# The second of two MLPs in blocks of 768 tokens, its first layer by Strassen's algorithm; its weights widened earlier, attention's steps further apart

## Chip, cores and metric

One core of a Trainium2 chip runs the whole program. The metric is the device time of one execution, in microseconds. PE is TensorE, DVE VectorE, ACT ScalarE, POOL GpSimd; SP issues the DMAs.

## The reference

Linear attention over 8 batches, 8 heads, 576 tokens of 64 channels, then two MLPs over the 4608 tokens of 512 channels, with 2048 channels between. Weights come as float64.

```python
def _attn_ref(q, k, v):
    q_s = np.exp(q - np.max(q, axis=-1, keepdims=True))
    q_s = q_s / (np.sum(q_s, axis=-1, keepdims=True) + 1e-09)
    k_s = np.exp(k - np.max(k, axis=2, keepdims=True))
    k_s = k_s / (np.sum(k_s, axis=2, keepdims=True) + 1e-09)
    kv = np.einsum('bhsd,bhse->bhde', k_s, v)
    return np.einsum('bhsd,bhde->bhse', q_s, kv)
...
x = attn_out.transpose(0, 2, 1, 3).reshape(B * S, H * D)
h = x @ w_in;  r = np.maximum(h, 0.0);  y = (r * r) @ w_out            # first MLP
h = y @ w_in2;  g = h * (1.0 / (1.0 + np.exp(-1.702 * h)));  out = g @ w_out2
```

## The kernel before

Every large product takes both operands as hi + lo (hi rounded to float32r, lo the rest) and adds three products, hi hi, hi lo and lo hi, in PSUM. So one step of either layer on a 128x128 piece of weights is three matmuls of 512 columns. Tokens go through in 9 blocks of TB = 512. For each block and each of 16 chunks f of the middle channels, `first` (L450) makes 12 matmuls into a tile `ph`, `steps_g` (L468) turns it into g (ACT's Relu or Sigmoid L475/L477, a DVE multiply L483, `to_hi` on ACT L120, `to_lo` on POOL L123), and `second` (L497) adds 12 matmuls into four `acc` banks, LAG = 2 chunks behind. The first MLP runs over all blocks and leaves y in DRAM; `plan_y` brings it back for the second MLP, which runs the same loops.

PSUM has eight banks: four for `acc`, two for `ph` (pool `ps_h`), two for attention (`ps_at`).

Attention works on a pair of heads at a time, one block ahead of the MLP. Its steps, with the names used below: km (DVE, maximum over k), pt (PE transposes km), mt (DVE), pb (PE spreads mt), ke (DVE subtracts, ACT takes exp), pk (PE, k times v), r, kvn, kvh, kvl; and for q: qs (DVE maximum and sum), POOL's subtraction and multiplication, qt (16 DVE transposes, L377), qh (ACT), ql (DVE), px (PE, L414), xh and xl. Per block there are four pairs.

Weights are widened from float64 words by `steps_w` (L136): a load, ACT's Abs (L160), three DVE bit steps (L165, L168, L171), then hi on ACT and lo on POOL. Those of the second MLP follow during block 8 and after it, in the place of the first MLP's.

The order is written in two ways. Up to block 1 it is the hand-written list ORDER. After that each step has a time in us (`at`), counted in half slots HS = 2.6, and steps are emitted in order of time; the lists KV1, X1 and W1 (L98 to L100) hold the times of attention's steps and of the weights. Each engine runs its instructions in that order. SP issues all DMAs, in order, and waits there for what a DMA needs.

## Time and profile before

| | us |
|---|---|
| median of 3 runs (lowest to highest) | 1727.88 (1727.25 to 1729.3) |
| span of the profiled execution | 1726.0 |
| PE busy in it | 1677.2 (97%) |
| DVE, ACT, POOL busy | 770.9, 594.2, 562.0 |
| PE's chain: first layers L460, second layers L509 | 37%, 35% of the span |

The page is one execution. Matmuls overlap in it: a matmul of 512 columns is listed with 0.39 us, and the next starts 0.23 us after it, so counts in a window say more than durations. "Idle before" is the time that an engine stood still ahead of an instruction, with what ended it.

### The profile page before, as it was taken

How to read it: one execution, taken by the hardware profiler on the slowest of the kernel's cores; microseconds unless marked ns; L12 is line 12 of the kernel's file. 1: busy time of each engine (PE TensorE's matmuls, PEld its weight loads, DVE VectorE, ACT ScalarE, POOL GpSimd, SP SyncE). 2: the span in 40 equal slices, each digit the busy share in tenths (PEclk: the TensorE clock that was granted, in tenths of full speed). 3: DMA queues.
4: the chain of work that ended last, by engine and by line, in shares of the span. 5: the costliest groups of instructions: out<-in, count | busy, mean ns of one | idle time of the engine just before them, and what ended most of it. 6: DMA issues, size and time to landing. Idle time of an engine off the chain costs nothing.

```text
span 1726.0 us, 19815 instructions
## 1 busy us (share of the span) xinstructions
PE 1677.2 (97%) x7560; PEld 1384.2 (80%) x7560; DVE 770.9 (45%) x1360; ACT 594.2 (34%) x1030; POOL 562.0 (33%) x470
## 2 busy tenths in 40 slices
PE   6789999999999999999999999999999999999999
PEld 5568888888888888878887888888888888888887
DVE  8995555656554655544368752121212121212111
ACT  5654333333333333333245432222222222222222
POOL 4665323333233323323245542222222222222222
PEclk9989999999999999999999999999999999999999
DMA  7552212121110202110234420000101010101000
GB/s 208 163 148 85 52 27 67 38 63 42 47 44 24 81 27 60 28 37 13 79 92 143 129 80 22 26 24 22 29 15 35 8 42 2 48 1 43 1 25 25
DMA packets 103712, 92.52 MB, mean 54 GB/s; under 512 B 51905, under 2 KB 85697, under 8 KB 103617
## 3 DMA queue, kind: packets, MB, share of 16 engines
q1 hardware_dynamic: 103616, 91.25, 18.0%
q8 instruction: 59, 0.97, 0.2%
q14 instruction: 37, 0.29, 0.1%
HBM read 72.35 MB, written 18.87 MB: 53 GB/s over the span
## 4 chain that ended last, share of the span: by engine, by line
PE 74%; DVE 17%; ACT 4%; issue 3%; DMA 1%; POOL 1%; SPq 0%; DVEq 0%; ACTq 0%; POOLq 0%
PE ph L460 37%; PE acc L509 35%; DVE qt L377 6%; DVE ql L123 2%; DVE to L168 1%; PE px L414 1%; ACT qh L120 1%; DVE ti L168 1%; DVE g L483 1%; DVE to L165 1%; DVE ti L165 1%; DMA rawi<-in_moe_w_in_dram 1%; ACT kvn L297 1%; DVE ti L171 1%; ACT g L475 1%
## 5 line engine op out<-in xcount | busy, mean ns | idle before, releaser
L123 POOL TENSOR_TENSOR g<-g,g 128x512 fp32r<-128x512 f32 x288 | 377.6, 1311 | 986.1 <-ACT g L120 887.1
L460 PE MATMUL ph<-xh,wih 128*128 128x512 f32 x1152 | 453.8, 394 | 0.1
L460 PE MATMUL ph<-xl,wih 128*128 128x512 f32 x1152 | 449.1, 390 | 0.4 <-DVE xl L123 0.4
L460 PE MATMUL ph<-xh,wil 128*128 128x512 f32 x1152 | 449.3, 390 | 0.0
L509 PE MATMUL acc<-g,woh 128*128 128x512 f32 x1152 | 361.6, 395 | 2.5 <-ACT g L475 1.8
L509 PE MATMUL acc<-woh,g 128*128 128x512 f32 x1152 | 356.7, 391 | 3.8 <-ACT o L523 3.8
L483 DVE TENSOR_TENSOR g<-ph,g 128x512 f32<-128x512 f32 x144 | 99.6, 692 | 528.4 <-ACT g L477 525.9
L120 ACT ACTIVATE g<-g 128x512 fp32r<-128x512 f32 x288 | 182.0, 632 | 274.5 <-DVE g L483 274.4
L509 PEld LDWEIGHTS acc<-woh,g 128*128 128x128 f32 x1152 | 217.3, 189 | 49.7 <-ACT o L523 4.2
L460 PEld LDWEIGHTS ph<-xh,wih 128*128 128x128 f32 x1152 | 217.1, 188 | 45.6 <-PE warm L594 0.2
L460 PEld LDWEIGHTS ph<-xh,wil 128*128 128x128 f32 x1152 | 216.6, 188 | 45.8
L509 PEld LDWEIGHTS acc<-g,woh 128*128 128x128 f32 x1152 | 214.1, 189 | 48.4 <-ACT g L475 2.7
L460 PEld LDWEIGHTS ph<-xl,wih 128*128 128x128 f32 x1152 | 216.8, 188 | 44.0 <-DVE xl L123 0.7
L477 ACT ACTIVATE g<-ph 128x512 f32<-128x512 f32 x144 | 86.1, 598 | 422.8 <-PE ph L460 422.8
L509 PE MATMUL acc<-g,wol 128*128 128x512 f32 x576 | 225.6, 392 | 0.5 <-POOL wol L123 0.5
L509 PE MATMUL acc<-wol,g 128*128 128x512 f32 x576 | 225.1, 391 | 0.0
L483 DVE TENSOR_TENSOR g<-g 128x512 f32<-128x512 f32 x128 | 91.8, 717 | 202.1 <-ACT g L475 199.7
L475 ACT ACTIVATE g<-ph 128x512 f32<-128x512 f32 x144 | 85.9, 597 | 217.2 <-PE ph L460 215.9
L377 DVE STREAM_TRANSPOSE qt<-q 32x128 f32<-32x128 f32 x448 | 135.5, 303 | 7.9 <-POOL q L352 2.2
L509 PEld LDWEIGHTS acc<-g,wol 128*128 128x128 f32 x576 | 108.6, 189 | 24.3 <-POOL wol L123 1.0
L509 PEld LDWEIGHTS acc<-wol,g 128*128 128x128 f32 x576 | 108.6, 189 | 22.5
L123 DVE TENSOR_TENSOR xl<-yr,xh 128x512 fp32r<-128x512 f32 x36 | 45.6, 1267 | 43.7 <-ACT xh L120 43.7
(67 smaller groups left out, 1124.1 us busy)
## 6 DMA issues: line engine op xcount, KB each, us to landing
rawi<-in_moe_w_in_dram SPq DMA_DIRECT2D x32, 512.0 KB, 3.8
rawo<-in_moe_w_out_dram SPq DMA_DIRECT2D x32, 512.0 KB, 3.6
...
```

What stands on the lines that cost most here:

```text
L120: nc.scalar.activation(hi, src, AF.Copy)
L123: eng.tensor_tensor(out=lo, in0=src, in1=hi.bitcast(F32), op=ALU.subtract)
L165: nc.vector.tensor_scalar(out=t, in0=t, scalar1=3, scalar2=1, op0=ALU.logical_shift_left, op1=ALU.bitwise_or)
L168: nc.vector.scalar_tensor_tensor(out=t, in0=high, scalar=-0x80000000, in1=t, op0=ALU.bitwise_and, op1=ALU.bitwise_or)
L171: nc.vector.scalar_tensor_tensor(out=t, in0=low, scalar=29, in1=t, op0=ALU.logical_shift_right, op1=ALU.bitwise_or)
L297: nc.scalar.activation(kn[hs, hs], pk[hs, hs], AF.Copy, scale=r[hs])
L377: nc.vector.transpose(out=st["qt"][32 * g : 32 * g + 32, a * P : (a + 1) * P].rearrange("d (j t) -> d j t", j=QJ), in_=st["qn"][32 * a : 3 ...
L460: nc.tensor.matmul(ph, a[:, cs], x[:, c, :], start=(c == 0 and e == 0), stop=(c == NC - 1 and e == 2),)
L475: nc.scalar.activation(st["g"], st["h"], AF.Relu)
L477: nc.scalar.activation(st["g"], st["h"], AF.Sigmoid, scale=1.702)
L483: nc.vector.tensor_tensor(out=st["g"], in0=st["g"] if m == 0 else st["h"], in1=st["g"], op=ALU.mult)
L509: nc.tensor.matmul(acc, lhsT, rhs, start=(f == 0 and e == 0), stop=(f == NF - 1 and e == 2),)
```

## The change

**Second MLP.** Its tokens go in 6 blocks of 768 (two halves of TH = 384). The first layer takes the products of 2x2 blocks (two halves of the tokens, two halves of the input channels, two chunks of 128 middle channels) with seven block products in place of eight (`steps_l1`). One such piece of work, "a quad" here (`quad(n)`, n from 0 to 47), has seven products of six matmuls of 384 columns, spaced by PT = QT / 7 in the plan. Sums of x (s1 to s4, `steps_s`) and of weights (a, b, `steps_q`) are made once and split in hi and lo. Results are put together by DVE adds as the products appear (c11, c12, c21, c22), in two `ps_h` banks in turn. `unit` is one piece of the second layer: three matmuls of 512 columns; 12 of them, for the quad before, lie between the products. Six accumulators hold 768 tokens, the two attention banks being free by then.

**Weights of the second MLP** are widened during blocks 1 to 7 (`steps_w` with m = 1) and stored in DRAM as float32; block 8 loads those of the first layer, makes their sums and splits them. Those of the second layer are split in quads 0 to 7, stored as hi and lo, and loaded again for each later block of tokens (`load_o`).

**Attention.** KV1 and X1 have longer distances, and x of a block lies once, not twice, in SBUF: px is copied out (`x_out`) and split into hi and lo (`split_x`) just ahead of the block.

```diff
-    KV1 = [HS * t for t in (-4, -3.9, -0.9, 0.2, 1.1, 2.2, 3.1, 3.15, 4.2, 5.1, 5.1, 5.1, 5.1)]
-    X1 = [HS * t for t in (-2, 0.1, 0.1, 1.1, 2.1, 2.1, 3.6, 5.1, 5.1, 6.2, 7.1, 7.1)]
-    W1 = [HS * t for t in (-4, -1, 0, 1, 1)]
+    KV1 = [HS * t for t in (-4, -3.9, -0.9, 0.6, 1.5, 2.7, 3.5, 3.55, 5.6, 6.6, 6.6, 6.6, 6.6)]
+    X1 = [HS * t for t in (-2, 0.1, 0.1, 1.1, 2.1, 2.1, 4.0, 6.0, 6.0, 8.2, 9.0)]
+    QT = 15.4
+    PT = QT / 7
...
-    xpool = ctx.enter_context(tc.tile_pool(name="xpool", bufs=2))
+    xpool = ctx.enter_context(tc.tile_pool(name="xpool", bufs=1))
...
+    raws = Places(
+        [(wpool, f"i{NF - 5 - e}") for e in range(4)]
+        + [(wpool, f"o{NF - 1 - e}") for e in range(4)]
+        + [(xpool, "x6"), (cpool, "raw")]
+    )
...
+    def split_x(i, p):
+        new_x(i, p)
+        src = x_t.pop(("f", i, p))
+        to_hi(x_t[i, p][:, 0, :], src)
+        to_lo(x_t[i, p][:, 1, :], src, x_t[i, p][:, 0, :], nc.gpsimd if p % 2 else nc.vector)
...
+        def product(bank, x, begin):
+            def run():
+                if begin:
+                    st[bank] = ps_h.tile([P, TB], F32, tag="h", name=f"p{x}_{n}")
+                a, at0 = W_AT[x]
+                w, xs = wt[a, j], x_t["2", i, x]
+                for k in range(2):
+                    cs = slice(at0 + k * P, at0 + (k + 1) * P)
+                    three(st[bank][:, :TH], lambda e: w[:, e, cs], lambda e: xs[:, e, k, :], begin and k == 0, k == 1, shared=True)
...
+        return [
+            (0.0, product(0, "a11", True)),
+            (0.48, m1),
+            (1.0, product(1, "s2", True)),
+            (1.5, add("c12", 1, "m1")),
+            (2.0, product(0, "a12", False)),
+            (2.5, act("c11")),
+            (3.0, product(1, "s3", False)),
+            (3.1, split("c11")),
+            (3.5, add("c22", 1, "m1")),
+            (4.0, product(0, "s1", True)),
+            (4.5, add("c22", 0, "c22")),
+            (4.55, act("c22")),
+            (5.0, product(1, "a22", False)),
+            (5.1, split("c22")),
+            (5.5, add("c21", 1, "m1")),
+            (5.55, act("c21")),
+            (6.0, product(0, "s4", False)),
+            (6.1, split("c21")),
+            (6.5, add("c12", 0, "c12")),
+            (6.55, act("c12")),
+            (7.1, split("c12")),
+        ]
...
+        for n in range(2 * NF):
+            i, e = (1 + n // 5, n % 5) if n < 20 else (5 + (n - 20) // 4, (n - 20) % 4)
+            t = slot(i) + (4.2 + (5.6 if n < 20 else 6.8) * e) * HS
+            when(t, [HS * e for e in (0, 3.0, 3.4, 4.2, 5.0, 5.1)], steps_w("io"[n // NF], 1, n % NF))
...
+            at(t + 2.1 * HS, sums("a"))
+            at(t + 3.1 * HS, sums("b"))
+            for e, a in enumerate(("w1", "wa", "wq", "wb")):
+                if a != "wb" or j % 2 == 0:
+                    f, tag = next(tags)
+                at(max(t + (2.2 + 0.9 * e) * HS, slot(NB - 1, f + 1) + HS), split(a, tag))
...
+            else:
+                t = quad(NQ * i - 1)
+                times = [quad(NQ * i - 6) - t, quad(NQ * i - 3) + 0.7 * PT - t, quad(NQ * i - 2) + 0.7 * PT - t]
+                times += [0.6 * PT if i < 2 else quad(NQ * i - 2) + 3.7 * PT - t]
+                times += [e * PT for e in (0.5, 1.55, 2.55, 1.6, 3.6, 4.6, 5.6, 6.6)]
+                when(t, times, steps_s(i))
+        UNITS = [0, 0, 1, 1, 2, 2, 3, 3, 4, 4, 5, 6]
```

Three places of the order follow. The first is DVE, one pair of heads (attention for block 3, while the MLP is in block 2; g is the MLP's square, ti a weight being widened). DVE's rows before:

```order
L263 TENSOR_TENSOR ke_1_2587<-k_1_2387,pb_1_2568 128x2x5x64
L483 TENSOR_TENSOR g_2_6_2593<-g_2_6_2593 128x512
L377 STREAM_TRANSPOSE qt_1_2599<-q_1_2467 32x128 x16
L290 TENSOR_SCALAR r_1_2650<-pk_1_2628 128x1
L291 RECIPROCAL r_1_2650<-r_1_2650 128x1
L123 TENSOR_TENSOR ql_1_2660<-qt_1_2599,qh_1_2659 128x4x4x32
L483 TENSOR_TENSOR g_2_7_2663<-g_2_7_2663 128x512
L238 TENSOR_REDUCE km_2_2681<-k_2_2583 128x128
```

DVE's rows after, for the same pair, from the square of g5 on:

```order
L635 TENSOR_TENSOR g_5_2638<-g_5_2638 128x512
L414 TENSOR_TENSOR ke_1_2644<-k_1_2426,pb_1_2616 128x2x5x64
L528 STREAM_TRANSPOSE qt_1_2659<-q_1_2501 32x128 x16
L635 TENSOR_TENSOR g_6_2692<-g_6_2692 128x512
L137 TENSOR_TENSOR ql_1_2719<-qt_1_2659,qh_1_2718 128x4x4x32
L201 TENSOR_SCALAR ti_6_2704<-ti_6_2704 128x512
L389 TENSOR_REDUCE km_2_2723<-k_2_2631 128x128
L441 TENSOR_SCALAR r_1_2725<-pk_1_2698 128x1
```

The transposes stand ahead of the square of g6 that they followed, r and its reciprocal went behind ql, and a bit step of a weight (ti) came between ql and the next pair's km.

The second place is PE in the second MLP. Its rows before (ph the first layer, acc the second):

```order
L460 MATMUL ph_2_9_9238<-xh_2_8439,wil_9_7889 128x512
L460 MATMUL ph_2_9_9238<-xh_2_8439,wih_9_7887 128x512
L460 MATMUL ph_2_9_9238<-xl_2_8440,wih_9_7887 128x512
L460 MATMUL ph_2_9_9238<-xh_2_8439,wil_9_7889 128x512
L509 MATMUL acc_2_0_9022<-woh_7_7759,g_1_2_7_9190 128x512 x2
L509 MATMUL acc_2_0_9022<-wol_7_7761,g_1_2_7_9190 128x512
L509 MATMUL acc_2_1_9023<-woh_7_7759,g_1_2_7_9190 128x512 x2
```

PE's rows after, the first four products of quad 5 (pa and ps the products, gc the results of quad 4 that the second layer takes):

```order
L610 MATMUL pa_5_8650<-a_0_7544,w_7822 128x384 x6
L610 MATMUL acc_0_0_8147<-wo_0_8_8592,gc_4_8581 128x512 x3
L610 MATMUL acc_0_1_8151<-wo_0_8_8592,gc_4_8581 128x512 x3
L610 MATMUL ps_5_8670<-s_0_7592,wq_7865 128x384 x6
L610 MATMUL acc_0_2_8164<-wo_0_8_8592,gc_4_8581 128x512 x3
L610 MATMUL acc_0_3_8168<-wo_0_9_8622,gc_4_8619 128x512 x3
L610 MATMUL pa_5_8650<-a_0_7988,w_7822 128x384 x6
L610 MATMUL acc_0_4_8183<-wo_0_9_8622,gc_4_8619 128x512 x3
L610 MATMUL acc_0_5_8187<-wo_0_9_8622,gc_4_8619 128x512 x3
L610 MATMUL ps_5_8670<-s_0_7997,wa_7828 128x384 x6
```

Rows of 12 and 12 matmuls became products of six matmuls of 384 columns with one or two units of three matmuls of 512 between them.

The third place is POOL in block 8. Its rows before (g the lo part of the MLP's g, wol and wil of a weight):

```order
L123 TENSOR_TENSOR g_0_8_8_7320<-g_8_8_7317,g_0_8_8_7320 128x512
L123 TENSOR_TENSOR wol_1_7346<-to_1_7296,woh_1_7344 128x512
L123 TENSOR_TENSOR g_0_8_9_7367<-g_8_9_7364,g_0_8_9_7367 128x512
L123 TENSOR_TENSOR wil_2_7388<-ti_2_7340,wih_2_7386 128x512
L123 TENSOR_TENSOR g_0_8_10_7413<-g_8_10_7410,g_0_8_10_7413 128x512
L123 TENSOR_TENSOR wol_2_7418<-to_2_7370,woh_2_7416 128x512
L123 TENSOR_TENSOR wil_3_7454<-ti_3_7406,wih_3_7452 128x512
```

POOL's rows after, in the same block (w, wa, wq and wbb are the lo parts of the weights and of their sums):

```order
L137 TENSOR_TENSOR wq_7620<-tb_7575,wq_7620 128x512
L137 TENSOR_TENSOR g_8_7_7641<-g_7_7638,g_8_7_7641 128x512
L137 TENSOR_TENSOR wbb_7656<-tt_7503,wbb_7656 128x256
L137 TENSOR_TENSOR w_7659<-tt_7595,w_7659 128x512
L137 TENSOR_TENSOR g_8_8_7684<-g_8_7681,g_8_8_7684 128x512
L137 TENSOR_TENSOR wa_7699<-ta_7636,wa_7699 128x512
L137 TENSOR_TENSOR wq_7702<-tb_7662,wq_7702 128x512
L137 TENSOR_TENSOR wbb_7656<-tt_7595,wbb_7656 128x256
```

Between two lo parts of g stand one or two weight splits before, and two or three after.

## Rows read from the trace of the kernel before

**Rows 1.** The page, part 1: busy time of each engine (share) xinstructions.

```profile
PE 1677.2 (97%) x7560; PEld 1384.2 (80%) x7560; DVE 770.9 (45%) x1360; ACT 594.2 (34%) x1030; POOL 562.0 (33%) x470
```

**Rows 2.** Windows: busy us (xinstructions) of each engine, granted clock, DMA.

```profile
core 0: us, PE busy (x) PEld busy (x) DVE busy (x) ACT busy (x) POOL busy (x), PEclk, DMA share, GB/s
50.00:100.00 50.00, 39.47 (x165) 30.84 (x164) 49.00 (x56) 28.68 (x53) 32.64 (x24) 0.93 0.53 153
300.00:400.00 100.00, 98.51 (x465) 81.73 (x464) 54.49 (x126) 37.03 (x66) 31.35 (x29) 1.00 0.18 48
900.00:1000.00 100.00, 96.23 (x413) 79.15 (x412) 80.71 (x91) 49.41 (x86) 55.88 (x40) 0.97 0.44 137
1100.00:1200.00 100.00, 100.00 (x442) 82.79 (x442) 19.78 (x25) 25.86 (x43) 24.10 (x19) 1.00 0.07 22
```

**Rows 3.** Waits of PE, 150 to 850 and 850 to 1000: total, times, longest.

```profile
PE px L414 <- DVE ql L123: 10.0, 19, 0.6
...
PE acc L509 <- ACT o L523: 3.8, 1, 3.8
```

**Rows 4.** Timeline of one pair of heads, 388 to 402.

```profile
388.36 0.27 PE L252 MATMUL pb<-ident,mt 128*128 128x128 f32 x1
...
392.81 5.04 DVE L377 STREAM_TRANSPOSE qt<-q 32x128 f32<-32x128 f32 x16
...
399.21 1.11 ACT L120 ACTIVATE qh<-qt 128x512 fp32r<-128x512 f32 x1
...
400.35 1.09 DVE L123 TENSOR_TENSOR ql<-qt,qh 128x512 fp32r<-128x512 f32 x1 [2.11 <-ACT qh L120]
...
400.65 0.28 PE L414 MATMUL px<-qh,kvl 128*128 128x256 f32 x1
...
401.50 0.38 PE L414 MATMUL px<-ql,kvh 128*128 128x256 f32 x1 [0.57 <-DVE ql L123]
```

**Rows 5.** Timeline of PE: px with 384 columns, then 512 (203 to 206.5).

```profile
204.70 0.34 PE L414 MATMUL px<-qh,kvh 128*128 128x384 f32 x1
...
205.22 0.40 PE L460 MATMUL ph<-xh,wih 128*128 128x512 f32 x1
...
205.91 0.39 PE L460 MATMUL ph<-xh,wih 128*128 128x512 f32 x1
```

**Rows 6.** Timeline of weight loads (PEld) in px, 301.9 to 304.2.

```profile
303.21 0.19 PEld L414 LDWEIGHTS px<-ql,kvh 128*128 128x128 f32 x1 [0.76 <-DVE ql L123]
303.32 0.19 PEld L414 LDWEIGHTS px<-qh,kvh 128*128 128x128 f32 x1
```

**Rows 7.** Timeline of PE behind the wait at the passage, 943 to 946.6.

```profile
943.84 1.22 PE L509 MATMUL acc<-woh,g 128*128 128x512 f32 x2 [3.77 <-ACT o L523]
...
945.28 1.06 PE L509 MATMUL acc<-woh,g 128*128 128x512 f32 x2
```

**Rows 8.** Timeline of DVE and POOL while weights are widened, 880 to 889.

```profile
882.66 0.69 DVE L168 SCALAR_TENSOR_TENSOR ti<-rawi,ti 128x512 int32<-128x512 int32 x1
883.04 1.47 POOL L123 TENSOR_TENSOR g<-g,g 128x512 fp32r<-128x512 f32 x1 [3.08 <-ACT g L120]
...
883.39 1.67 DVE L171 SCALAR_TENSOR_TENSOR ti<-rawi,ti 128x512 int32<-128x512 int32 x1
...
884.47 1.75 POOL L123 TENSOR_TENSOR wol<-to,woh 128x512 fp32r<-128x512 f32 x1
```

**Rows 9.** Costliest groups: busy us, mean ns of one, idle before.

```profile
L123 POOL TENSOR_TENSOR g<-g,g 128x512 fp32r<-128x512 f32 x288 | 377.6, 1311 | 986.1 <-ACT g L120 887.1
L120 ACT ACTIVATE g<-g 128x512 fp32r<-128x512 f32 x288 | 182.0, 632 | 274.5 <-DVE g L483 274.4
...
L238 DVE TENSOR_REDUCE km<-k 128x128 f32<-128x640 f32 x32 | 41.7, 1303 | 1.3 <-DMA k<-in_k_dram 1.3
L168 DVE SCALAR_TENSOR_TENSOR to<-rawo,to 128x512 int32<-128x512 int32 x32 | 38.0, 1187 | 1.1
L171 DVE SCALAR_TENSOR_TENSOR to<-rawo,to 128x512 int32<-128x512 int32 x32 | 32.7, 1023 | 1.1
L165 DVE TENSOR_SCALAR to<-to 128x512 int32<-128x512 int32 x32 | 26.4, 825 | 6.7 <-ACT to L160 6.7
```

More of the change, by code (lines that the diff above doesn't have):

```diff
@@ L468, in steps_g, with three, first @@
-    def steps_g(m, i, f):
+    def three(out, w, x, start, stop, shared=False):
+        for e, (a, b) in enumerate(((0, 0), (0, 1), (1, 0))):
+            nc.tensor.matmul(
+                out, w(a), x(b), start=(start and e == 0), stop=(stop and e == 2), skip_group_check=shared
+            )
+    def first(i, f, chunks=range(NC)):
+        if chunks[0] == 0:
+            pool, tag = (ps_acc, f"acc{f}") if i == 0 and 2 <= f < OPEN else (ps_h, "h")
+            h_t[i, f] = pool.tile([P, TB], F32, tag=tag, name=f"ph{i}_{f}")
+        w = wt["i", f]
+        for c in chunks:
+            x, cs = x_t[i, c], slice(c * P, (c + 1) * P)
+            three(h_t[i, f], lambda e: w[:, e, cs], lambda e: x[:, e, :], c == 0, c == NC - 1)
@@ new lines, in put @@
+    def put(i):
+        if i < NB - 1:
+            both = cpool.tile([P, 2, TB], F32, tag="raw", name=f"o{i}")
+        for c in range(NC):
+            if c > 1 and i < NB - 1:
+                o = both[:, c - 2, :]
+            else:
+                o = cpool.tile([P, TB], F32, tag="tgtg"[c], name=f"o{i}_{c}", bufs=2)
+            if c % 2 == 0:
+                nc.scalar.activation(o, acc_t[i][c], AF.Copy)
+            else:
+                nc.vector.tensor_copy(o, acc_t[i][c])
+            nc.sync.dma_start(out=y_d[i][:, c, :], in_=o)
@@ new lines, with put_2 @@
+    at_once = []
+    more_o = {}
+    def put_2():
+        for i, tokens in at_once:
+            acc = acc_t["2", i][tokens][0]
+            if i < NB2 - 1 and tokens not in (2, 3):
+                o = late["pool"].tile([P, TB], F32, tag="o", name=f"o2_{i}_{tokens}", bufs=2)
+            elif i < NB2 - 1:
+                if tokens == 2:
+                    more_o[i] = cpool.tile([P, 2, TB], F32, tag="raw", name=f"o2_{i}")
+                o = more_o[i][:, tokens - 2, :]
+            else:
+                if i not in more_o:
+                    more_o[i] = late["pool"].tile([P, NT2, TB], F32, tag="xf", name=f"o2_{i}")
+                o = more_o[i][:, tokens, :]
+            if tokens % 2 == 0:
```

556 lines of the change are left out of this document (374 added, 182 removed).

## The prediction

> **What bounds the kernel now.** I read the page first, then the table of windows, the waits and the timelines. TensorE is busy for 1677.2 of the 1726.0 us [rows 1]. The windows say where the rest lies. In the second MLP (1100 to 1200) TensorE is busy all the time: 442 matmuls of 512 columns, one per 0.2262 us, at a granted clock of 1.00 [rows 2]. There only fewer columns can save time. In the first MLP (300 to 400) 1.5 us of 100 are lost; at the passage between the MLPs (900 to 1000) 413 matmuls ran where 442 fit, 29 x 0.2262 = 6.6 us; up to 150 VectorE is the bound (49.00 of 50 us) [rows 2]. The waits name the first two losses [rows 3]. From 150 to 850 the one wait is px for ql, 19 times, 10.0 us. Near 940 the one wait is acc for ACT's copy o, 3.8 us, and behind it matmuls run at half clock: a pair takes 1.06 us where 0.62 is usual [rows 7], which is the rest of the 6.6.
>
> **1. First layer of the second MLP.** Before: 9 x 16 x 12 = 1728 matmuls of 512 columns. After, by the code and the order: 48 units of work ("quads": 768 tokens, 256 channels) with seven products of 6 matmuls of 384 columns, 2016 in all. The second layer keeps its 1728 matmuls of 512. What does one of 384 columns cost? The trace has them, in threes, in px: starts at 204.70 and 205.22 are three apart, 0.173 us each; right behind, three of 512 columns (205.22 to 205.91) are 0.230 apart [rows 5]. The ratio is 0.7536, near 3/4, so I see no fixed part, and take 0.7536 x 0.2262 = 0.1704. Sum: 1728 x 0.2262 = 390.9 before, 2016 x 0.1704 = 343.5 after, **-47.4 us**. Bounds: -48.8 at exactly 3/4, -41.5 at 0.1733.
>
> Twice as many small accumulations need readers in between. In a quad PE runs product, units of the second layer (two, two, two, two, two, one, one, of 3 x 0.2262 = 0.68 us each), product of 1.02 us, and so on: 7 x 1.02 + 12 x 0.68 = 15.3 us. A product that goes on in a bank, or takes its buffer again, comes two steps behind the one before in it, so reader chains have 3.7 us (1.36 + 1.02 + 1.36), and 2.4 us (0.68 + 1.02 + 0.68) at the tightest, add c21 before the next quad's a11. An add of 384 columns is 3/4 of the 0.69 us of a 512 step [rows 8], 0.5 us as an estimate. That is covered, so the products cost nothing beyond their columns in an ordinary quad. In quad 0 there is no second layer of its own to fill in: after s3 ends, act c11 (sigmoid and multiply, about 1.2 us) has one product of 1.02 as cover, and add c21 similar: 0.3 + 0.3, with hand-overs **+1** (0 to 3).
>
> **2. Attention's steps spread.** The chain of one pair of heads now [rows 4]: pb at 388.36; 16 transposes on DVE from 392.81, 5.04 us; qh on ACT until 400.32; ql on DVE until 401.44; px waits, its third matmul starts 0.85 us after the second where 0.11 is usual. PE has four half slots of 12 matmuls (2.72 us each) and pk between pb and px. The order shows six after the change, 6 x 2.72 + 0.55 = 16.9 us. DVE's row there: square of g5 (waits for ph5: 2.72 + 0.7 + 0.7, so 4.2 us after pb), ke until 5.0, transposes until 10.0, square of g6 10.7, then ql, when qh (11.1) is there, until 12.3. So 4.6 us of cover, and the px waits go: 10.0 us by the waits, 19 x 0.74 = 14 by the starts, I take **-13**.
> What is late next: km of the next pair stands behind ql, and now behind b0 of a widened weight too (0.83 us), and takes 1.30 [rows 9]: done at 14.4, pt's turn on PE at 5 x 2.72 + 0.55 = 14.15. In that pair (one of four, in blocks 1 to 7) PE waits 0.2 us, or 1.2 if DVE has met a POOL step: **+1.5** (0 to 7 x 1.2 = 8). The other pairs have over 1 us left by the same count.
>
> **3. Weights widened in blocks 1 to 7.** The 32 chunks (on DVE 0.83 + 1.19 + 1.02 [rows 9]) are not more work, but move out of block 8 and beyond, where DVE was busy 80.71 of 100 us, into blocks where it is busy 54.49 [rows 2]: five of 3.0 us per block of some 95 us (384 x 0.2262 and attention's products), about 70. Hidden beside TensorE, but for the km above. Their loads and stores go through SP: a store waits there for DVE's last bit step, and loads of k and q queue behind it. Those loads are issued at least 2.1 half slots (5.5 us) ahead of use; I count nothing, up to 2.
> x has one buffer now. Block i's x is split after first(i-1,15) has read each quarter: two ACT steps of 0.63 and DVE or POOL steps of 1.3 per pair, while PE has 2.0 + 2.7 us before first(i,0) starts and 0.68 more per quarter: nothing, by 0.7 us at the least.
>
> **4. Block 8 and the passage.** The old wait of 3.8 with its half-clock stretch goes (**-6.6**), since its copies are no longer behind weights. But POOL and DVE now share block 8 with 32 splits, 16 g_lo, and the sums of x. The trace shows that steps of these two hold each other up where both DVE operands are in SBUF: an L171 of 0.69 us that begins during a POOL step ends 0.55 after that step (1.67), and the POOL step behind it takes 1.75 [rows 8]. Work: POOL 40 x 1.29 + 8 x 0.65 + three of 768 columns at 1.94 = 62.6; DVE squares 16 x 0.69, sums 8 x 1.43, three of 768 at 1.0 = 25.5; together 88.1 against 16 x 5.43 = 86.9 us of the block. As the rows hand over 0.14 us early each time, it is rather 77. g_lo has 10.9 us from ph to its use, less 0.63 + 0.69 + 0.63 + 1.31 [rows 9]: 7 us of cover for a backlog. I take **+1.5** for the last splits (a12, s1, s4 stand behind wa and wq on POOL), 0 to 7.
> The Trainium skill's page "SBUF — State Buffer" (section "SBUF: two separate sides") gives the rule: the pair of ports is an exclusive lock, held for the whole instruction. Rows 8 agree, with 1.67 for 0.69. By that rule at its full durations block 8 would be oversubscribed.
>
> **5. Boundaries of the 768-token blocks.** In quads 7, 15, 23, 31, 39 POOL has 4 x 0.98 + 4 x 1.94 = 11.7 us of 15.3 (quad 7 with two weight splits 14.3), and DVE's multiplies and x sums wait among them. The chain multiply c22, add c21, multiply c21, add c12 then ends about when the bank is wanted: **+3** (0 to 10).
>
> **6. Start and end.** DVE, the bound there, loses three subtractions of 0.69: **-1** (0 to -4, as raw weights have ten places in place of three). The end (last copy and store) is the same.
>
> **Sum** on the profiled execution: 1726.0 - 47.4 + 1 - 13 + 1.5 - 6.6 + 1.5 + 3 - 1 = 1665.0. The median of the runs shown, 1727.88, is 1.9 above that span: **1667 us**.
>
> **The rivals.**
> Ports: POOL and DVE hold each other up in block 8 and at the boundaries beyond their cover, PE stops for some us and then runs at half clock as at 943.84 [rows 7]. Price: 6.6 again at the passage, 5 x 2 at the boundaries, less the 4.5 already counted: 1679. For it: 88.1 of 86.9 above. Against: the 7 us of cover.
> Refill: the px waits come back elsewhere (km, mt, or a load behind a store on SP), as DVE goes from 54 to 70: +13, 1680. Against: the spread moves each of these steps apart too.
> Weight loads: each load lasts 0.19 us [rows 6], more than the 0.170 of a matmul of 384 columns; if it set the pace, 2016 x (0.188 - 0.1704) = +35, 1702. Against: in rows 6 loads of 0.19 start 0.11 apart, so they overlap. The page "Perfetto Trace Analysis" of the Trainium skill (section "Identifying the Most-Contended Engine") judges TensorE by the share of LDWEIGHTS; by it the second MLP would go from 83% to 78 x 0.188 / 15.3 = 96% and have little left, but no run yet shows such loads in a long row.
> Slower: in every quad PE waits for a bank, because a multiply with two SBUF operands meets a POOL step (1.6 in place of 0.5) ahead of add c21 and add c12, whose cover is 2.4 us. Slower than before from (1731 - 1667) / 48 = 1.35 us a quad; at 1.4 it is 1734. For it: rows 8. Against: POOL has 4 us of 15.3 in an ordinary quad.
> That the change doesn't do what it says is excluded: the order has 2016 matmuls of 384 columns and 1728 of 512 fewer.
>
> **How the numbers follow.** Forecast 0.67, ports 0.13, refill 0.08, weight loads 0.05, slower 0.05, and 0.02 for some sum of losses that ends within 0.2% (3.5 us, about what a measurement of this kernel can tell from no change). Low end: -48.8, -14, -6.6, -4, nothing new: 1654. High end: 0.1733 (+5.8), px only 10 (+3), attention +5, ports +12: 1693. Faster 0.93, same 0.02, slower 0.05.
>
> **What would show it.** Right: matmuls of 384 columns 0.170 apart in the second MLP, a quad in 15.3 us, no wait of px for ql after 200, nothing over 1 us at the passage. Wrong: 0.188 in their place; waits of PE for DVE's c or POOL's g in every quad; waits of pt for km; a granted clock under 1.00 near the passage.

## The result, and the profile of the changed kernel

The changed kernel takes 1698.15 us (median of 4 runs, 1697.46 to 1700.28), the kernel before 1727.57 on the same chip: a ratio of 0.9831, 95% interval 0.9817 to 0.9845. It is faster by 29.4 us, where 61 were forecast. The profiled execution has a span of 1696.8 us; the sum had given 1665.0. So 31.8 us are to be found.

The page's first part has TensorE busy for 97% of the span and VectorE, the next of the engines beside it, for 55%; it stands against [rows 1]:

```profile
PE 1645.3 (97%) x7848; PEld 1411.2 (83%) x7848; DVE 940.5 (55%) x1647; ACT 669.6 (39%) x1228; POOL 694.7 (41%) x589
```

The windows, in the columns of [rows 2], tell the stages apart. They are, in this order, attention beside the first MLP, the passage in two halves, and the second MLP:

```profile
300.00:400.00 100.00, 98.65 (x469) 81.87 (x468) 71.43 (x146) 41.15 (x74) 34.49 (x30) 1.00 0.29 86
850.00:900.00 50.00, 45.77 (x193) 36.80 (x192) 23.55 (x23) 17.45 (x33) 32.59 (x26) 0.97 0.20 68
900.00:950.00 50.00, 45.81 (x208) 39.16 (x207) 30.54 (x29) 23.82 (x44) 42.01 (x31) 0.97 0.26 85
1100.00:1200.00 100.00, 100.00 (x500) 89.93 (x498) 40.81 (x65) 35.85 (x68) 39.10 (x32) 1.00 0.21 77
```

In the second MLP TensorE never waits, and still does only 500 matmuls in 100 us: a quad has 78, so it takes 15.6 us, not 15.3. The timeline of TensorE there shows why (start, us, engine, line, operation, count):

```profile
1299.68 1.21 PE L610 MATMUL ps<-s,wa 128*128 128x384 f32 x6
1300.72 1.55 PE L610 MATMUL acc<-wo,gc 128*128 128x512 f32 x6
1302.11 1.21 PE L610 MATMUL ps<-s,wa 128*128 128x384 f32 x6
```

From start to start, six of 384 columns take 1300.72 - 1299.68 = 1.04 us, and six of 512 take 1.39. Over the stretch of 1120 to 1680 the mean from start to start is 0.1749 us at 384 columns and 0.2317 at 512, where the sum had 0.1704 and 0.2262. Both kinds of matmul became dearer.

The waits of PE, first 150 to 850, then 850 to 1000, against [rows 3] (total, times, longest):

```profile
PE pt L395 <- DVE r L441: 3.4, 6, 0.8
PE pt L395 <- DVE km L389: 2.6, 1, 2.6
...
PE pa L610 <- DVE c L796: 4.0, 1, 4.0
PE ph L610 <- ACT g L629: 3.1, 1, 3.1
PE acc L610 <- POOL g L137: 0.9, 1, 0.9
```

The px waits for ql are gone, waits of pt stand in their place, and the passage has two new waits of 3 and 4 us, each with a stretch at the lower of TensorE's two clock levels (1.2 for 2.4 GHz) behind it: the granted clock is 0.97 in both halves of the passage.

So the missing time lies in four places, by starts in the trace:

| stage | forecast | measured | missing |
|---|---|---|---|
| second MLP, 2016 x 0.1749 + 1728 x 0.2317 | 734.4 | 753.0 | 18.6 |
| passage and quad 0, above pure streams | 2.5 | 13.2 | 10.7 |
| attention, 150 to 850: 40 matmuls more than before, x 0.2262 | -11.5 | -9.0 | 2.5 |
| start, 0 to 150: 6 matmuls fewer | -1 | +1.3 | 2.3 |

The forecast of 2.5 for the passage is the +1.5 for the last splits and the +1 for quad 0. The four give 34.1, some 2 more than the 31.8 that are missing; I can't place those 2.

### The profile page after: what moved, and what is told of

The parts are those of the page before. It is cut to its first block, busy times and chain, and to the rows that moved or that the text cites. A ratio compares the mean times of both kernels' runs of the same rounds, so it can differ in the third digit from the quotient of the medians.

```text
span 1696.8 us, 21565 instructions
## 1 busy us (share of the span) xinstructions
PE 1645.3 (97%) x7848; PEld 1411.2 (83%) x7848; DVE 940.5 (55%) x1647; ACT 669.6 (39%) x1228; POOL 694.7 (41%) x589
## 5 line engine op out<-in xcount | busy, mean ns | idle before, releaser
L610 PE MATMUL acc<-wo,gc 128*128 128x512 f32 x1728 | 453.9, 394 | 0.0
L610 PE MATMUL acc<-g,wo 128*128 128x512 f32 x1728 | 425.2, 395 | 4.2 <-ACT g L629 1.6
L610 PE MATMUL ph<-x,wi 128*128 128x512 f32 x1728 | 425.4, 395 | 3.5 <-ACT g L629 3.1
L610 PEld LDWEIGHTS acc<-g,wo 128*128 128x128 f32 x1728 | 323.4, 190 | 74.0 <-POOL g L137 2.9
L610 PEld LDWEIGHTS ph<-x,wi 128*128 128x128 f32 x1728 | 322.6, 189 | 71.8 <-ACT g L629 3.5
L137 POOL TENSOR_TENSOR gc<-c,gc 128x384 fp32r<-128x384 f32 x192 | 199.5, 1040 | 437.4 <-ACT gc L134 430.5
L610 PEld LDWEIGHTS acc<-wo,gc 128*128 128x128 f32 x1728 | 319.8, 188 | 46.3
L137 POOL TENSOR_TENSOR g<-g,g 128x512 fp32r<-128x512 f32 x144 | 194.4, 1350 | 396.9 <-ACT g L134 352.2
L610 PE MATMUL pa<-a,w 128*128 128x384 f32 x576 | 117.7, 339 | 4.4 <-DVE c L796 4.0
L610 PE MATMUL ps<-s,wa 128*128 128x384 f32 x576 | 116.0, 335 | 0.7 <-DVE c L808 0.4
L610 PEld LDWEIGHTS ps<-s,wa 128*128 128x128 f32 x576 | 102.8, 188 | 10.2 <-DVE c L808 1.2
```

The costliest lines, as they stand in the source:

```text
L137: eng.tensor_tensor(out=lo, in0=src, in1=hi.bitcast(F32), op=ALU.subtract)
L610: nc.tensor.matmul(out, w(a), x(b), start=(start and e == 0), stop=(stop and e == 2), skip_group_check=shared)
```

## Experiments

The runs were made on several chips, on which the kernel before took 1726.9 to 1729.1 us. So each time is compared with that of the kernel before on the same chip ("difference"). A difference has an uncertainty of some 2.5 us, so where less is at stake I go by the traces.

### The price of a matmul in the second MLP

**e1: streams alone.** This program has nothing but matmuls, in rows of one width, then in the order of two quads, alone and beside each other engine.

> The kernel is left out but for its matmul shapes: TensorE runs streams of F32R matmuls one after the other, each from a line of its own, and no result is the reference's. Streams: 512 columns 12 to a bank; 384 columns 6 to a bank; 384 columns out of 512-wide operands; 512 columns 3 to a bank with weights out of a 384-wide tile; the products and units of two quads in the order of the changed kernel (84 of 384, 72 of 512), alone, with four units at a time, beside ScalarE, VectorE, GpSimd, and all three with transfers. Theory A (the price lies in TensorE's own stream): in the quads alone the mean start to start is 174 to 176 ns at 384 columns and 231 to 233 at 512, as in the changed kernel, while the pure streams stay near 170 and 226; the neighbours add nothing. Theory A' (the price comes from the neighbours): the quads alone run at 170.4 and 226.5 ns, 15.2 us a quad, and some 4 ns a matmul appear only in the streams beside ScalarE, VectorE, GpSimd or transfers, and that stream names the neighbour.

The timeline of TensorE: L63 and L68 are the 384 columns (L68 out of 512-wide operands), L73 the 512 in threes, L79 and L82 the two quads that begin at 100.44 and end at 129.03, where L88 starts:

```profile
45.33 16.83 PE L63 MATMUL bank<-x,W 128*128 128x384 f32 x96
62.00 16.80 PE L68 MATMUL bank<-X,W 128*128 128x384 f32 x96
78.64 21.96 PE L73 MATMUL bank<-W,G 128*128 128x512 f32 x96
100.44 2.27 PE L79 MATMUL bank<-x,W 128*128 128x384 f32 x12
102.54 1.55 PE L82 MATMUL bank<-W,G 128*128 128x512 f32 x6
...
129.03 3.30 PE L88 MATMUL bank<-x,W 128*128 128x384 f32 x18
```

A pure row of 384 takes (62.00 - 45.33) / 96 = 0.1736 us each, one of 512 (100.44 - 78.64) / 96 = 0.2271. In the quads, with no other engine at work, the means are 0.1749 and 0.2317: those of the changed kernel to the last digit. Beside ScalarE, VectorE, GpSimd and all three with transfers they stay at 0.1748 to 0.1749 and 0.2317 to 0.2318. Theory A holds in that the price lies in TensorE's own stream, and A' falls; but A had the pure rows near 170 ns, and 384 columns stand at 173.6 there. Four units at a time instead of two (L88 and L91) gave 0.1752 and 0.2300, so coarser groups win next to nothing.
The Trainium skill's page "SBUF — State Buffer" (section "SBUF: two separate sides") says that TensorE's own ports never wait for another engine; this run agrees, with 0.1749 us alone and 0.1748 to 0.1749 beside the others.

**e8: what in the order costs.** These are streams of the same kind, with one thing changed at a time.

> Only matmul streams again, no result: 512 and 384 columns alone; 6 and 6, 12 and 12, 24 and 24, 3 and 3, 42 and 36 of each in turn; the same alternation of operands and banks with both kinds at 512 columns, and with both at 384; 256 with 512 and 448 with 512. Theory (each change of width costs a fixed sum, some 35 to 45 ns for a pair of changes, spread over the first 9 or so matmuls behind it): the alternation at one width runs at the pure 227 and 173.5 ns; per pair of changes the excess is the same at 12 and at 24 and smaller where runs are shorter than 9; with 42 and 36 the mean comes within 1 ns of the pure streams. Rival (the price comes of changing operands or banks, not width): the alternations at one width show it too, 174.9 and 231.7 ns.

The timeline: L64 and L133 are the pure rows of 384 and 256, L69 and L72 six and six, L77 and L80 the same change of operands and banks with both at 512:

```profile
58.06 16.83 PE L64 MATMUL bank<-x,W 128*128 128x384 f32 x96
74.73 1.20 PE L69 MATMUL bank<-x,W 128*128 128x384 f32 x6
75.77 1.55 PE L72 MATMUL bank<-W,G 128*128 128x512 f32 x6
77.16 1.21 PE L69 MATMUL bank<-x,W 128*128 128x384 f32 x6
...
103.92 1.53 PE L77 MATMUL bank<-X,W 128*128 128x512 f32 x6
105.29 1.52 PE L80 MATMUL bank<-W,G 128*128 128x512 f32 x6
106.65 1.52 PE L77 MATMUL bank<-X,W 128*128 128x512 f32 x6
...
310.19 11.68 PE L133 MATMUL bank<-x,W 128*128 128x256 f32 x96
321.71 1.55 PE L138 MATMUL bank<-x,W 128*128 128x384 f32 x8
```

At one width the change of operands and banks costs nothing: groups of six start 1.36 to 1.37 us apart. With a change of width the six of 512 take 1.39. Means from start to start, in ns:

| in turn | 384 | 512 | above pure rows, per pair of changes |
|---|---|---|---|
| alone | 173.6 | 226.7 | |
| 3 and 3 | 175.9 | 232.1 | 23 |
| 6 and 6 | 174.0 | 231.5 | 31 |
| 12 and 12 | 175.1 | 230.1 | 59 |
| 24 and 24 | 174.4 | 228.4 | 60 |
| 42 and 36 | 173.8 | 227.8 | 48 |

So it is the width, as the theory said. But a pair of changes costs 48 to 60 ns where the runs are 12 or longer, not 35 to 45, and 42 and 36 came within 1.1 ns, just outside the 1 ns that the theory allowed.

The pure rows hold a second finding. 256, 384 and 512 columns take 119.9, 173.6 and 226.7 ns (the first is (321.71 - 310.19) / 96, rounded). The steps are 53.7 and 53.1 for 128 columns, so the line through them is 0.417 ns a column, one column per cycle at 2.4 GHz, and 13 ns that each matmul pays at all three widths. That is the fixed part which the prediction did not see.
The Trainium skill's page "TensorE: Matmul & The Clock Gate" (section "Back-to-back issue gap") has the same slope and 2.5 ns of fixed part for an isolated matmul; here the slope agrees and the fixed part is 13.

### The spread of attention's steps and the widening of weights

**e4, e6, e14.** e4 has the lists KV1 and X1 as before. e6 is e4 without VectorE's three bit steps on the weights of the second MLP, and e14 is the changed kernel without them:

```diff
-    KV1 = [HS * t for t in (-4, -3.9, -0.9, 0.6, 1.5, 2.7, 3.5, 3.55, 5.6, 6.6, 6.6, 6.6, 6.6)]
-    X1 = [HS * t for t in (-2, 0.1, 0.1, 1.1, 2.1, 2.1, 4.0, 6.0, 6.0, 8.2, 9.0)]
+    KV1 = [HS * t for t in (-4, -3.9, -0.9, 0.2, 1.1, 2.2, 3.1, 3.15, 4.2, 5.1, 5.1, 5.1, 5.1)]
+    X1 = [HS * t for t in (-2, 0.1, 0.1, 1.1, 2.1, 2.1, 3.6, 5.1, 5.1, 6.2, 7.1)]
...
-                st["bits"][e]()
+                if m == 0:
+                    st["bits"][e]()
```

> The changed kernel with the steps of attention in blocks 2 to 8 at the times that they had before (KV1 and X1), all else as changed. Theory D (the spread of the steps ended px's waits for ql and is worth the 9 to 12 us by which the stretch of 150 to 850 us became shorter): those waits of about 2 us are there again, the waits of pt for the maximum that came with the spread are gone, and the time is 8 to 13 us above the changed kernel's, 1706 to 1711. Rival (the waits went because the refill's work moved out of those blocks and the widening of weights took its place): 1696 to 1700.

> The kernel with attention's steps at the old times, in which VectorE's three operations on each of the second MLP's widened weights are left out (those weights are wrong then; loads, ScalarE's part and stores stay). With the old times the changed kernel took 1726.9 us. Theory (it is the widening, some 8 to 9 us of VectorE in each 100, that makes the old times so dear: by itself it costs some 20 us and the spread hides it): 1704 to 1710, and px's and pt's waits in 150 to 850 us are back at about the 22 us that the kernel before has above its pure streams. Rival (the widening is harmless, and the earlier start of each block's steps or the x tiles in one buffer make the waits): 1720 to 1727.

> The changed kernel with its own times, in which VectorE's three operations on each widened weight of the second MLP are left out in blocks 1 to 7 (those weights are wrong then; loads, ScalarE's part and stores stay). With the old times these operations cost 14 us (1726.9 against 1712.8). Theory (at the new times they lie in VectorE's slack, as the prediction had it): 1696 to 1698.5, 150 to 850 us as long as in the changed kernel within 1.5 us. Rival (they still cost, through r and km behind them on VectorE): pt's waits for r go, 1692 to 1695.

| attention's times | bit steps | us | difference to before | matmuls in 150 to 850 |
|---|---|---|---|---|
| old | made | 1726.88 | -0.3 | 3121 |
| old | left out | 1712.76 | -16.3 | 3189 |
| new | made | 1698.15 | -29.4 | 3247 |
| new | left out | 1697.26 | -29.7 | 3250 |
| kernel before | not there yet | | 0 | 3207 |

With the old times the changed kernel is as slow as the one before: without the spread the change is worth nothing. The waits of e4 in 150 to 850 say where it goes:

```profile
PE px L565 <- DVE ql L137: 7.2, 13, 0.6
PE pt L395 <- DVE km L389: 5.3, 5, 2.6
PE px L565 <- ACT qh L134: 4.4, 5, 1.3
PE acc L610 <- DVE o L666: 4.4, 7, 1.1
```

e4's ten runs lie between 1719.06 and 1729.15 us, and e6 and e14 ran once each, so the matmuls in the traces are the surer measure. In the old order the bit steps cost 68 matmuls, 15.4 us; in the new one 3, 0.7 us. The spread by itself, without them, is worth 13.4 us (-16.3 to -29.7), with them 29.1. Theory D had the mechanism and a price that was far too low, because it left this out. e6 came out above its range (1712.8 for 1704 to 1710): px's waits are there, and acc's for VectorE's copy o, 4.4 us, which the kernel before does not have in [rows 3] and whose cause I did not follow.

### The passage

The trace of the changed kernel shows two stalls. This is the first, 866 to 882:

```profile
867.42 1.85 POOL L712 TENSOR_TENSOR xf<-xf 128x768 f32<-128x768 f32 x1
...
869.21 2.30 POOL L137 TENSOR_TENSOR a<-xf,a 128x768 fp32r<-128x768 f32 x1
...
869.74 2.32 DVE L635 TENSOR_TENSOR g<-g 128x512 f32<-128x512 f32 x1
...
875.36 0.95 DVE L310 TENSOR_TENSOR tb<-tt,ta 128x256 f32<-128x256 f32 x1 [3.29 <-POOL wq L137]
...
878.62 0.84 ACT L134 ACTIVATE s<-xf 128x768 fp32r<-128x768 f32 x1 [4.55 <-DVE xf L712]
879.37 0.58 ACT L629 ACTIVATE g<-ph 128x512 f32<-128x512 f32 x1
...
880.01 2.48 PE L610 MATMUL ph<-x,wi 128*128 128x512 f32 x7 [3.08 <-ACT g L629]
```

A square of 0.69 us takes 2.32 beside GpSimd's 768-wide steps; VectorE then waits 3.29 us for GpSimd to free a tile for tb, ScalarE 4.55 for VectorE's sum, and the Relu that TensorE needs stands behind that on ScalarE's queue. The second, 936 to 943:

```profile
936.01 0.73 POOL L137 TENSOR_TENSOR wbb<-tt,wbb 128x256 fp32r<-128x256 f32 x1
...
936.77 1.69 SPq L272 DMA_DIRECT2D to<-wod  x2
...
939.90 0.63 ACT L134 ACTIVATE wo<-to 128x512 fp32r<-128x512 f32 x1 [4.00 <-DMA to<-wod]
940.43 0.51 ACT L807 ACTIVATE s<-c 128x384 f32<-128x384 f32 x1
...
942.80 1.65 PE L610 MATMUL pa<-a,w 128*128 128x384 f32 x4 [4.01 <-DVE c L796]
```

The load of to goes out when GpSimd's wbb frees its tile; ScalarE waits 4.00 us for it, with the sigmoid that the products need behind it in its queue.

**e2, e3, e5: one stall each, then both.** In e2 the load of to0 goes into another pool's tile and is issued early; in e3 the sums of x are set apart in block 8; e5 has both:

```diff
-            st["t"] = cpool.tile([P, 2, DM], F32, tag="raw", name=f"to{n}")
+            pool, tag = (gpool, "g") if n == 0 else (cpool, "raw")
+            st["t"] = pool.tile([P, 2, DM], F32, tag=tag, name=f"to{n}")
...
-            when(quad(n), [PT * e for e in (2.0, 3.7, 5.2)], steps_o(n))
+            when(quad(n), [PT * e for e in (2.0 if n else 0.2, 3.7, 5.2)], steps_o(n))
...
-                times = [e + 4 * HS, e + 8 * HS, e + 9.5 * HS, e + 11.5 * HS, e + 10 * HS, e + 12 * HS]
-                times += [slot(NB) - HS, e + 13 * HS, m, m, m + HS, m + HS]
+                times = [e + t * HS for t in (4, 9.3, 13.3, 21.3, 17.3, 25.3)]
+                times += [slot(NB) - HS, e + 28.5 * HS, m, m, m + HS, m + HS]
```

> The changed kernel with the first load of the widened second-layer weights (tile to0) in a tile of its own pool slot, issued at the start of the first quad and no longer behind GpSimd's release of the tile that both used. Theory B (the second stall of the passage, 4.18 us of TensorE and about 2 us at half clock behind it, is ScalarE waiting for this load): the wait of pa for VectorE near 938 us goes, and the time is 5 to 7 us below the changed kernel's, 1691.5 to 1693. Rival (ScalarE and VectorE are late there in any case, because GpSimd and VectorE still work off block 8): ScalarE's wait for the transfer goes but another takes its place, and less than 2 us is won.

> The changed kernel with the six sums and splits of the first 768-token block that stood within 5 steps of block 8 (s1 8, s3 9.5, a11 10, s2 11.5, s2s 12, s4 13, in half slots of 2.6 us) set apart (9.3, 13.3, 17.3, 21.3, 25.3, 28.5). Theory C (the stall at 872 to 880 us comes of these six standing together, on GpSimd and VectorE which hold each other up): TensorE's waits of 4.2 us at 875 to 880 us and the half clock behind them go, 5 to 7 us less, 1691 to 1693. Rival (block 8 as a whole asks too much of GpSimd and VectorE): the waits move to a later place in block 8, and the time stays within 2 us of 1698.

> Both edits of the passage in one kernel: tile to0 loaded early in a slot of its own, and the six sums and splits of the first 768-token block set apart in block 8. Alone they gave 3.5 us and nothing; the second took the stall of 876 us away and TensorE lost the same time 55 us later, at half clock behind two waits of 1.7 and 4.1 us. Theory (the two stalls have causes of their own, and the half clock behind the second was the price of the late load): 8 to 9 us below the changed kernel, 1689 to 1690.5. Rival (the work that GpSimd and VectorE owe is only pushed along, and is paid in the first quad whatever comes first): as with the early load alone, 1693.5 to 1695.

e2: 1694.66, difference -32.6, 3 us better than the change, between theory B's 5 to 7 and the rival's 2; the wait falls from 4.0 to 1.1, with a new one of 0.7 for ScalarE's copy m. e3: 1698.19, difference -29.0, nothing gained, as its rival said; its longer waits in 850 to 1000 are

```profile
PE pa L610 <- DVE c L796: 3.9, 1, 3.9
PE ps L610 <- DVE c L808: 1.6, 1, 1.6
```

The wait of ph for g is gone, and 1.6 us came up at 931, close to the wait of 3.9. The granted clock, 0.83 in 880 to 890 of the changed kernel, is 1.00 there now, and 0.83 and 0.66 in 930 to 940 and 940 to 950, where it was 1.00 and 0.83. So the low clock moved with the waits, and the time was given back 50 us later. e5: 1693.98, difference -35.1, in matmuls of 850 to 960 (table below) 27 more than the change. The time lies in the rival's range; by the difference and the matmuls it is 2.5 us better than e2, between theory and rival. What the rival says is in its window of 890 to 940:

```profile
890.00:940.00 50.00, 47.77 (x214) 38.87 (x213) 40.53 (x34) 24.28 (x45) 48.46 (x33) 1.00 0.20 69
```

GpSimd is busy 48.46 of 50 us: in this stretch it has no room left, and spreading only moves its work about.

**e9, e10, e13: work taken from GpSimd.** The low parts of block 8's weight splits are made on VectorE: all 32 on top of e5 (e9), 16 of them on top of e5 (e10), or all 32 and nothing else (e13). (The expectations count 28 and 12; by the pages' numbers of instructions it is 32 and 16.)

```diff
                 to_hi(w[:, 0, :], src)
-                to_lo(w[:, 1, :], src, w[:, 0, :], nc.gpsimd)
+                to_lo(w[:, 1, :], src, w[:, 0, :], nc.vector)
```

> The kernel with both edits of the passage (early to0, sums set apart), and the low parts of all 28 splits of the second MLP's combined first-layer weights in block 8 (w1, wa, wq, wbb) taken from GpSimd to VectorE. From 890 to 940 us GpSimd was busy 48.5 of 50 us there, and VectorE 40.5. Theory (GpSimd owes more in block 8 than it has time for, and the first quad pays: alone such an operation takes 1.28 us on GpSimd and 0.69 on VectorE): the waits of 930 to 950 us, some 4 us, go: 1688 to 1691. Rival (VectorE is as full, since the two hold each other up whenever both read their operands from the buffer): VectorE is late with the squares of block 8, TensorE waits there for g, and the time is 1695 to 1710.

> As the run before this, but with the low parts of w1 and wbb alone on VectorE (12 of the 28). Theory: GpSimd is no longer full from 890 to 940 us, the waits of 930 to 950 us shrink to below 2 us: 1689 to 1692. Rival: VectorE's order holds the squares up: 1694 to 1700.

> The changed kernel with one edit only, the low parts of the 28 splits of block 8's combined weights on VectorE; to0 and the sums of the first 768-token block stay as the change has them. Theory (GpSimd's arrears are the common cause of both stalls of the passage: of the late squares at 876 us, and of the late load at 938 us, whose tile GpSimd's last split frees): both stalls go without the other two edits, 1689 to 1692. Rival (the two stalls have a cause each, and GpSimd's load only makes them longer): one of the waits of 3 and 4 us stays, 1693 to 1697.

The window of e9:

```profile
890.00:940.00 50.00, 47.76 (x221) 40.06 (x220) 38.25 (x50) 25.00 (x47) 22.48 (x16) 1.00 0.25 86
```

GpSimd falls from 48.46 to 22.48, and VectorE, with 16 operations more, from 40.53 to 38.25. VectorE's fall is one of this window alone: over 850 to 960 it rises from 63.59 to 72.02 us. Over the whole execution GpSimd loses 42.5 us and VectorE gains 10.2 against e5, from which only this edit parts it (the pages have 654.6 and 953.6 us for 697.1 and 943.4). So GpSimd was relieved of four times what VectorE took on; that the two then wait less for each other would explain it, but was not measured by itself. e9 takes 1690.24, difference -38.1; the theory held. e10 took 1694.61 (-33.7), no better than e5 and within its rival's range. In 890 to 940 GpSimd was busy only 34.12 of 50 us there, and TensorE made 199 matmuls where e5 made 214. So a full GpSimd alone is not what held the passage; in e10 TensorE waits 2.0 us for VectorE's c and 2.0 for GpSimd's g, and why half of the splits win nothing where all of them do is not shown. e13 took 1699.02 (-27.9), no better than the change and above both ranges. Its waits still say what its rival said, that the two stalls have a cause each:

```profile
PE pa L610 <- DVE c L796: 4.8, 1, 4.8
PE ph L610 <- ACT g L629: 1.7, 1, 1.7
```

GpSimd's splits are behind part of the first stall (3.1 to 1.7), not behind the second: there the load of to now goes out at 934.19, behind the stores of y on SP's queue, the last of which waited 3.5 us for VectorE's copy o. The late load has two causes in a row, and taking one away shows the other.

**e7, e16: the rest.** e7 put the two splits of to0 behind the sigmoids on ScalarE (4.7 and 6.2 for 3.7 and 5.2), and gave the first c11 another tile; e16 is e9 with the splits of a22 and s4 in quad 0:

```diff
-                times += [slot(NB) - HS, e + 28.5 * HS, m, m, m + HS, m + HS]
+                times += [slot(NB) - HS, e + 28.5 * HS, m, m, quad(0) + 1.6 * PT, quad(0) + 2.6 * PT]
```

> Both edits of the passage, and two more in the first quad: the two splits of tile to0 stand behind the sigmoids on ScalarE's queue (4.7 and 6.2 sevenths of the quad, from 3.7 and 5.2), and the first sigmoid's tile comes from the pair of c12's, not from the pair that the outputs of the block before are still being stored from. Theory (what is left of the passage is ScalarE's queue in order, a split or a store's release ahead of a sigmoid): 1 to 3 us below the kernel with the two edits alone, and no wait of TensorE above 1 us in 925 to 950 us. Rival (GpSimd's arrears of block 8 bound the first quad): the same time as with the two edits, within 1 us.

> Attention as in the changed kernel; in the passage all edits that helped: early to0, the sums set apart, the 28 low parts on VectorE, and the splits of a22 and s4 in the first quad. Theory (these add up to what the stretch of 850 to 960 us showed in the runs with each: 3.0 us above its pure streams, from 13.2): 1688 to 1690, some 9 us below the changed kernel. Rival (the time of 1690.2 with the splits at the old place is the floor that the first quad's own transfers set): 1690 to 1692.

e7 was worse than e5, 1696.89 (-32.2): TensorE waited for wo, 2.7 us for its low part and 1.2 for its high part, in quad 1. Both its hypotheses fell: the splits stood not too early but just in time. e16 took 1688.89 (-38.4), the same as e9 within the uncertainty, with 3 matmuls more in the window; that doesn't decide between its theory and its rival.

| | matmuls in 850 to 960 |
|---|---|
| changed | 449 |
| e3, e13, e7 | 451, 452, 458 |
| e2, e10, e5 | 465, 467, 476 |
| e9, e16 | 496, 499 |

From 449 to 499 are 50 matmuls, some 10 us at the 0.20 us of a mean one: nearly all of the 10.7 that the passage lost.

### The waits of pt

**e11, e12, e15, e17.** In e11 (on e5) r and what follows it come earlier, ahead of km. In e12 (on e9) and e15 (on e16) pt comes one group of matmuls later. In e17 (on e16) km comes earlier:

```diff
     KV1 of the changed kernel, of e11, of e12 and e15, of e17
     (-4, -3.9, -0.9, 0.6,  1.5, 2.7, 3.5, 3.55, 5.6, 6.6, 6.6, 6.6, 6.6)
     (-4, -3.9, -0.9, 0.6,  1.5, 2.7, 3.5, 3.55, 5.6, 6.0, 6.0, 6.0, 6.0)
     (-4, -3.9, -0.9, 1.05, 2.2, 2.7, 3.5, 3.55, 5.6, 6.6, 6.6, 6.6, 6.6)
     (-4, -3.9, -1.5, 0.6,  1.5, 2.7, 3.5, 3.55, 5.6, 6.6, 6.6, 6.6, 6.6)
```

> The kernel with both edits of the passage, and in attention's blocks 2 to 8 the reciprocal of the sum (r) and the three steps behind it at 6.0 half slots where they stood at 6.6, so that VectorE has r ahead of the next pair's maximum km (6.1) in its queue. Theory (pt's six waits of 0.4 to 1.0 us for r come of that order alone): they go, 150 to 850 us is 4 us shorter, 1689.5 to 1690.5. Rival (VectorE is busy with a widening there in any case, or km is then late by as much): the same time as the kernel with both edits within 1.5 us, pt waiting for km.

> The kernel with both edits of the passage and the 28 low parts on VectorE, and in attention's blocks 2 to 8 the transposition pt one matrix group later (1.05 half slots from 0.6, behind the second layer's group instead of ahead of it) with its maximum mt at 2.2 from 1.5. The attempt from the other side, r ahead of km, made VectorE wait for TensorE's pk and pt wait 1.0 to 3.2 us for km. Theory (pt stands too early for VectorE's order, in which km and r lie behind pk; a group of 2.7 us more covers both): the seven waits of pt, 6.0 us in all, go and nothing comes in their place: 1684 to 1686. Rival (mt and pb behind it become late, since VectorE waits for pt in the middle of its other work): pk or px wait instead, 1688 to 1696.

> The kernel with the late pt, the 28 low parts on VectorE and both edits of the passage, and the splits of a22 and s4 of the first 768-token block moved from the end of block 8 into the first quad (1.6 and 2.6 sevenths of it), where they are needed at 5 and 6. Theory (VectorE, busy 9.7 of 10 us at 920 to 930 us, holds up the products there): the waits of 926 to 938 us, some 2.5 us, shrink to below 1 us, 1 to 2.5 us below the kernel with the late pt. Rival (the transfers and splits of the first quad itself hold its products up): within 1 us of it.

> The kernel before it in this call, and in attention the maximum km 0.6 half slots earlier (1.5 ahead of its pair's start from 0.9), where VectorE stood idle for 2.3 us waiting for ScalarE's qh; r and pt stay. Both tries at pt's waits made them worse (r first: km late; pt later: mt late). Theory (pt waits because km runs behind ql and a widening, and r's place behind km only makes it look like r): the six waits, 4.4 us, go: 1684 to 1686. Rival (r itself, behind TensorE's pk, is what pt's buffer waits for): the waits stay, same time within 1 us.

The waits of PE in 150 to 850, in e11:

```profile
PE pt L396 <- DVE km L390: 13.1, 7, 3.0
```

In e12:

```profile
PE pb L404 <- DVE mt L400: 12.9, 14, 1.7
```

And in e17:

```profile
PE pt L396 <- DVE km L390: 2.6, 1, 2.6
```

e11 (1702.76, -25.6) made VectorE wait for TensorE's pk (6.6 us in 12 waits), with km behind it; e12 (1696.71, -30.2, where e9 has -38.1) turned the wait round, TensorE now waiting for mt; e15 (1696.09, -30.8) is e12 within its uncertainty. e17 took 1684.48, difference -42.8, 4.4 better than e16, as its theory said, and six of the seven waits are gone. The trace of the changed kernel puts those six down to r. Its DVE rows show how close the ends of km and r are:

```profile
299.71 1.09 DVE L137 TENSOR_TENSOR ql<-qt,qh 128x512 fp32r<-128x512 f32 x1 [2.27 <-ACT qh L134]
300.69 0.43 DVE L201 TENSOR_SCALAR ti<-ti 128x512 int32<-128x512 int32 x1
301.03 1.26 DVE L389 TENSOR_REDUCE km<-k 128x128 f32<-128x640 f32 x1
302.20 0.16 DVE L441 TENSOR_SCALAR r<-pk 128x1 f32<-128x1 f32 x1
```

km ends at 302.29 and r at 302.36; pt started at 302.44. VectorE had stood still for 2.27 us ahead of ql, and e17 put km into that hole. In e17's trace the same pair reads:

```profile
301.59 0.15 DVE L442 TENSOR_SCALAR r<-pk 128x1 f32<-128x1 f32 x1
301.99 0.27 PE L396 MATMUL pt<-ident,km 128*128 128x128 f32 x1
```

So r too came earlier, since km no longer stands ahead of it, and pt doesn't wait. This shows that km's 1.26 us at that place in VectorE's queue made the wait. The rival, by which r waits for TensorE's pk, falls. Whether pt waited for km or for r, e17 can't tell, as it moved both.

e17 beats both kernels: ratio to the kernel before 0.9749, 95% interval 0.9735 to 0.9762; 13.4 us below the changed kernel by differences.

## Why the prediction failed, step by step

**Step 1, first layer: right in kind, wrong in size, 18.6 of the 31.8 us.** The step that failed is "so I see no fixed part, and take 0.7536 x 0.2262". [Rows 5] held both numbers that were needed: 0.173 for a matmul of 384 columns and 0.230 for one of 512 right behind. The prediction took their ratio, and threw away that both stood above a pure stream's. Taken as they stand they give 2016 x 0.173 + 1728 x 0.230 = 746.2, which is 11.8 of the 18.6. In e8's terms, in ns a matmul, the 18.6 us are, to rounding, 2016 x (173.6 - 170.4) = 6.5 us for the fixed part, 0.9 for 226.7 in place of 226.2, and 2016 x 1.3 + 1728 x 5.0 = 11.3 for changes of width. Strassen's algorithm saves an eighth of the first layer's columns and adds a sixth to the number of its matmuls (2016 for 1728); that greater number has a price too. That the products wait for no bank, and that there is nothing else in a quad, was right: 100.00 of 100 us busy.

**The rival of weight loads** came to 1702, near the result, by another mechanism. Its price was 0.188 us a matmul; they stand 0.1749 apart, with loads of 0.19 us that overlap, and e8 shows no cost where only operands change. A near number is not a proof. Whether the fixed 13 ns have to do with the loads is open.

**Step 2, the spread: right in the main.** The px waits went and pt's wait came, once a block in six blocks, 3.4 us where 1.5 was taken and up to 8 allowed. Its reason was km in VectorE's queue, as named (e17); the widened weight ahead of km, on which the prediction's count rested, is only 1.0 us of it, as without the bit steps 2.4 us stay (e14). The spread alone is worth 13.4 us by e6 and e14, where -13 was written. That they agree so well is in part luck: in e6 px waits 6.7 us, not 10.0, and acc waits 4.4 us for VectorE's copy o, which the prediction didn't have. One more wait of 2.6 us, before 162, had not been seen. That the x tiles in one buffer cost nothing was not tried by itself.

**Step 3, the widening at no cost: right, for the times that the change gives it** (0.7 us in e14). The text named VectorE's slack as its cover, and that was not enough of a reason: at the old times, with no less slack (VectorE busy 453.52 of the 700 us from 150 to 850 in e4, 469.30 in the changed kernel), it costs 15.4 us (e4, e6). The cover is the place in VectorE's queue, not its idle share. The refill rival had this thought, and put 13 us on it.

**Step 4, the passage: wrong, 10.7 us.** The step that failed is the +1.5 for the last splits, argued from the 7 us of cover that g has. The arithmetic ahead of it, 88.1 us of work against 86.9 of the block, was the better guide; I argued it down to 77. And the cover was counted for one chain (ph to g), while the stalls came where queues cross. In the first, VectorE waits for a tile that GpSimd frees, ScalarE for VectorE, and TensorE for a Relu behind that on ScalarE's queue. In the second, which fell into quad 0 with its +1, a load waits for a release and a row of stores, and a sigmoid waits behind the load. The old wait of acc for o did go, as the -6.6 had it. The Ports rival named the place and the low clock behind it, at 12 us more than the forecast; the passage alone took nearly that.
The rule of the Trainium skill that the prediction set beside this (page "SBUF — State Buffer", section "SBUF: two separate sides", an exclusive lock for the whole instruction) would have block 8 oversubscribed. The trace agrees in part: e5's 48.46 of 50 us on GpSimd in 890 to 940 fits it, but over 850 to 960 GpSimd is busy 84.68 of 110, and e10 stalls with GpSimd at 34.12 of 50.

**Step 5, boundaries: right in the sum**, 2.9 us at quads 7 and 8 (1.6 of it in TensorE's waits from 1046 to 1062) and nothing at the later ones, for 3 at five of them. **Step 6, the start: wrong sign**, 1.3 us longer, with VectorE 6.5 us less busy in 0 to 150; it is small, and I did not look for its cause.
